# Which free PSUM bank an attention and MLP kernel takes: the one free longest in the preferred half in place of the one with the highest or lowest number

## The chip, the cores and the metric

The kernel runs on one core of a Trainium2 chip. The metric is the device time of one execution in microseconds (us), as the median of several runs.

TensorE (PE) multiplies matrices and writes the products into PSUM, an accumulator memory of eight banks; a bank holds 128 partitions of 512 fp32 numbers. VectorE (DVE) and ScalarE (ACT) read the products out of PSUM. GpSimd (POOL) helps with element-wise work, and SyncE (SP) issues the DMA transfers.

## The reference

Causal attention with a decay (8 batches, 8 heads, 576 tokens, head size 64), and then an MLP on its output, with a leaky ReLU between two matrix products:

```python
scores = scale * np.matmul(q, k.transpose(0, 1, 3, 2))
cum = np.cumsum(np.log(np.clip(f, 0.0001, 1.0)), axis=-1)
scores = np.where(causal, -1000000000.0, scores + cum[:, :, :, None] - cum[:, :, None, :])
attn = softmax(scores)                       # with 1e-09 in the sum
x = (attn @ v) as 4608 tokens of 512
h = x @ w_in                                 # 512 -> 2048
out = (max(h, 0) + alpha * min(h, 0)) @ w_out  # 2048 -> 512
```

The matrix products are made of several fp32r matmuls each (a high and a low part of either operand), so that the result has more than one pass's precision.

## The kernel before

**The stages.** Attention is cut into 32 units, each one batch and two heads. Units 0 to 9 transpose their exponentials on PE (`attention(n)`). Units 10 to 31 (`turned(n)`) transpose them on DVE (L863) and move the pieces with DMAs. A turned unit's work on PE is a first run of 18 score matmuls (`bank<-Qhl`, 64x512 and smaller), a second run of 12, and 60 matmuls that make the values (`bank<-big,vr`). DVE masks the scores (L840), ACT takes the exponentials (L820) and empties the values (L937).

**FFN1** (`ffn1(b)`, the first product of the MLP) has 9 token tiles of 512 tokens with 16 chunks each. A chunk is 12 matmuls of 128x512 at L377 (`bank<-xx,wi`), in two halves of 6, into one PSUM bank. Then the bank is read: for most tiles by ACT at L1014 and again by DVE at L1016, for the tiles of `LATE` (the first and the last two) by ACT at L1011 alone. The result `hs` goes out by a DMA. FFN1's chunks are set between the pieces of the attention units as soon as their tokens are there; after the last unit FFN1 runs alone, beside the preparation of w_out on ACT and DVE.

**FFN2** (`ffn2(u)`, the second product) has 18 units of 256 tokens. Each makes 168 matmuls of 128x256 (`bank<-wot,...` and `bank<-wi,...`) into four banks, which ACT (L1291) and DVE (L1295, L1296, L1299, L1300; in the last unit L1305 to L1308) read at the unit's end and sum.

**What sets the order.** The program is written by a planner in Python (`Plan.run`). It keeps a planned time for each engine, and in each step emits that operation which could start first by its own costs. The planned times are used only to choose; on the chip every engine runs its instructions in the emitted order and waits on semaphores. What an operation needs from a pool (a PSUM bank, a buffer) it takes when it is emitted: `Store.take(ring, now)`, where `st.free` holds pairs (planned time at which the item comes free, number). A `Ring` is one user's view of a store.

**PSUM banks.** The eight banks are one store, made of four tiles of two banks:

```python
two_banks = [psum.tile([128, 2, 512], F32, name=f"bank{i}") for i in range(4)]
banks = Store([t[:, i] for t in two_banks for i in range(2)])
rS, rT = Ring(banks, 2, 4, False), Ring(banks, 1, 3, False)
rH, rO = Ring(banks, 2, 4, True), Ring(banks, 0, 6)
rP, rV = Ring(pairs), Ring(banks, 0, 2, True)
```

Banks 0 and 1 are the first tile, 2 and 3 the second, 4 and 5 the third, 6 and 7 the fourth. The last argument is `high`: scores and transposes of the first units (`rS`, `rT`) prefer low banks, FFN1's chunks (`rH`) and the first units' values (`rV`) high ones, FFN2 (`rO`) has no preference. The framework sets the semaphore waits between operations that touch the same tile. With the first turned unit `swap_banks` takes banks 0 to 3 out of the store and gives them to the turned units as two pairs (`rP`); from there FFN1 has banks 4 to 7. `change`, after the attention, gives 0 to 3 back.

Of the kernel before, what the change touches and what calls it, by code (L numbers as in the profile page):

```python
# [48 lines left out]
class Store:  # L49
# [7 lines left out]
    def take(self, ring, now):  # L57

        near = [f for f in self.free if f[0] <= now]
        f = min(near, key=lambda f: (f[1] * (-1 if ring.high else 1))) if near and ring.high is not None else min(self.free)  # L60
        self.free.remove(f)
        return f

# [1313 lines left out]
```

## Time and profile before

| | us |
|---|---|
| median of 3 runs | 1164.29 |
| lowest and highest run | 1161.78, 1164.58 |
| the profiled execution | 1162.62 |
| its span, first to last instruction | 1160.4 |
| outside the span | 2.2 |
| PE busy | 1054.2 (91%) |
| DVE busy | 812.9 (70%) |
| ACT busy | 618.8 (53%) |
| POOL busy | 329.7 (28%) |

The mean clock that TensorE was granted is 0.997 of full speed.

How to read what follows: a chain of waits is followed back from the last instruction, at each step to what released it. "Idle before" is the time in which an engine stood still ahead of an instruction, with the instruction of another engine that ended it. A PE that is busy may still be filling or emptying its pipeline. In the names, `bank<-xx,wi` is output and inputs of an instruction, and L377 is the line of a helper through which almost all matmuls are issued, so that the operands tell the stages apart.

### The profile page before, as it was taken

How to read it: one execution, taken by the hardware profiler on the slowest of the kernel's cores; microseconds unless marked ns; L12 is line 12 of the kernel's file. 1: busy time of each engine (PE TensorE's matmuls, PEld its weight loads, DVE VectorE, ACT ScalarE, POOL GpSimd, SP SyncE). 2: the span in 40 equal slices, each digit the busy share in tenths (PEclk: the TensorE clock that was granted, in tenths of full speed). 3: DMA queues.
4: the chain of work that ended last, by engine and by line, in shares of the span. 5: the costliest groups of instructions: out<-in, count | busy, mean ns of one | idle time of the engine just before them, and what ended most of it. 6: DMA issues, size and time to landing. Idle time of an engine off the chain costs nothing.

```text
span 1160.4 us, 21964 instructions
## 1 busy us (share of the span) xinstructions
PE 1054.2 (91%) x7933; PEld 893.0 (77%) x7933; DVE 812.9 (70%) x1673; ACT 618.8 (53%) x1390; POOL 329.7 (28%) x459
## 2 busy tenths in 40 slices
PE   8889989889899989989898788889999999999998
PEld 4667767667677777777676565659899999999998
DVE  5678773657667575766665176659888898898894
ACT  5768786445454555555453154546545464545551
POOL 5577784435435353535442100000000000000000
PEclk9999999999999999999999999999999999999999
DMA  5867753666667667667666454436333434344421
GB/s 157 227 200 194 236 155 110 178 176 201 206 194 219 189 191 220 194 200 209 182 171 181 135 200 165 161 109 225 111 127 117 140 128 128 110 146 128 121 81 37
DMA packets 132879, 190.24 MB, mean 164 GB/s; under 512 B 21842, under 2 KB 78979, under 8 KB 132771
## 3 DMA queue, kind: packets, MB, share of 16 engines
q1 hardware_dynamic: 132482, 188.65, 53.4%
q8 instruction: 62, 1.02, 0.4%
q14 instruction: 47, 0.38, 0.1%
q10 hardware_dynamic: 288, 0.20, 0.1%
HBM read 103.52 MB, written 48.78 MB: 131 GB/s over the span
## 4 chain that ended last, share of the span: by engine, by line
PE 79%; DVE 10%; ACT 7%; issue 2%; DMA 1%; SPq 0%; DVEq 0%; POOL 0%; ACTq 0%; POOLq 0%
PE bank L377 76%; ACT hs L1014 2%; DVE hs L1016 2%; ACT hs L1011 2%; PE bank L586 2%; DVE big L863 1%; ACT big L582 1%; ACT big L573 1%; PE bank L437 1%; DVE big L699 1%; DMA Zt<-c 1%; DVE xx L1268 1%; DVE hs L1295 0%; PE bank L473 0%; DVE gh L1268 0%
## 5 line engine op out<-in xcount | busy, mean ns | idle before, releaser
L377 PE MATMUL bank<-xx,wi 128*128 128x512 f32 x1728 | 436.9, 401 | 77.1 <-DVE hs L1016 41.5
L377 PEld LDWEIGHTS bank<-xx,wi 128*128 128x128 f32 x1728 | 312.8, 188 | 175.2 <-DVE hs L1016 55.1
L1016 DVE SCALAR_TENSOR_TENSOR hs<-bank,sa,hs 128x512 f32<-128x512 f32 x96 | 71.5, 744 | 125.8 <-ACT hs L1014 64.8
L820 ACT ACTIVATE big<-big,st 128x512 f32<-128x512 f32 (+4 forms) x198 | 113.8, 577 | 77.6 <-DVE st L840 77.6
L541 POOL TENSOR_TENSOR Qhl<-rqk,Qhl 128x640 fp32r<-128x640 f32 (+1 forms) x56 | 87.2, 1560 | 214.8 <-ACT Qhl L540 214.8
L1014 ACT ACTIVATE hs<-bank,ab 128x512 f32<-128x512 f32 x96 | 65.9, 686 | 122.7 <-PE bank L377 107.5
L377 PE MATMUL bank<-wot,xx 128*128 128x256 f32 x1008 | 125.6, 284 | 6.1 <-DVE hs L1296 3.4
L377 PEld LDWEIGHTS bank<-wot,xx 128*128 128x128 f32 x1008 | 122.5, 192 | 7.9 <-DVE hs L1295 2.1
L377 PE MATMUL bank<-wi,xx 128*128 128x256 f32 x1008 | 124.1, 283 | 0.5 <-ACT hs L1291 0.5
L377 PEld LDWEIGHTS bank<-wi,xx 128*128 128x128 f32 x1008 | 122.3, 192 | 0.7 <-ACT hs L1291 0.7
L377 PE MATMUL bank<-Qhl 64*128 64x128 f32 (+4 forms) x840 | 97.7, 332 | 6.6 <-ACT wi L372 3.7
L377 PEld LDWEIGHTS bank<-Qhl 64*128 64x128 f32 (+1 forms) x840 | 77.0, 188 | 32.7 <-ACT xs L937 6.7
L377 PE MATMUL bank<-big,vr 128*64 128x128 f32 (+2 forms) x1880 | 97.0, 261 | 0.0
L377 PEld LDWEIGHTS bank<-big,vr 128*64 128x64 f32 x1880 | 90.1, 139 | 8.4 <-issue 4.7
L863 DVE STREAM_TRANSPOSE big<-big 128x2048 f32<-128x2048 f32 (+1 forms) x44 | 80.4, 1835 | 12.0 <-DMA big<-big 5.2
L840 DVE CUSTOM_DVE_ANT_1 big<-bank,Z 128x384 f32<-128x384 f32 (+1 forms) x88 | 39.6, 487 | 48.8 <-PE bank L377 48.8
L1265 ACT ACTIVATE xx<-gx 128x1024 fp32r<-128x1024 f32 x48 | 50.8, 1058 | 41.2 <-DVE gx L1252 27.9
L514 POOL TENSOR_TENSOR Z<-Z,tri 128x384 f32<-128x384 f32 x64 | 61.7, 968 | 29.0 <-DVE Z L498 12.1
L1011 ACT ACTIVATE hs<-bank,sg 128x512 f32<-128x512 f32 x48 | 33.0, 688 | 63.6 <-PE bank L377 59.8
L377 PE MATMUL bank<-wot,gh 128*128 128x256 f32 x504 | 63.4, 284 | 1.5 <-DVE hs L1296 0.8
L377 PEld LDWEIGHTS bank<-wot,gh 128*128 128x128 f32 x504 | 61.6, 192 | 2.4 <-DVE hs L1296 1.1
L1265 ACT ACTIVATE xx<-wx 128x256 fp32r<-128x256 f32 x68 | 33.9, 520 | 54.1 <-PE bank L377 34.2
(149 smaller groups left out, 1555.2 us busy)
## 6 DMA issues: line engine op xcount, KB each, us to landing
hd<-hs SPq DMA_DIRECT2D x144, 256.0 KB, 2.3
big<-big SPq DMA_DIRECT2D x352, 100.0 KB, 2.2
wx<-hd SPq DMA_DIRECT2D x45, 512.0 KB, 3.5
rqk<-in_qk_dram SPq DMA_DIRECT2D x28, 608.0 KB, 3.9
hr<-hd SPq DMA_DIRECT2D x27, 512.0 KB, 3.4
vr<-in_vv_dram SPq DMA_DIRECT2D x32, 320.0 KB, 3.0
big<-in_w_in_dram SPq DMA_DIRECT2D x16, 512.0 KB, 4.8
wr<-in_w_out_dram SPq DMA_DIRECT2D x16, 512.0 KB, 3.7
```

Of the source, the lines that this page charges most:

```text
L377: pe.matmul(o, lhsT, rhs, start=start, stop=stop)
L437: op("PE", 800, lambda: [pe.matmul(bw.t, wbf[:, 0:128], wbf, start=True, stop=True) for _ in range(3)], -200, [o_wbf], [bw])
L514: m1 = op("POOL", c_po(128 * 3), lambda z4=z4: po.tensor_tensor(z4()[:, 6:9], z4()[:, 0:3], tb(3), ALU.add), kc + 0.1, got + [o_mask], [bZ])
L541: o2 = op("POOL", c_po(w), lambda hi=hi, lo=lo, raw=raw: po.tensor_tensor(lo(), raw(), hi().bitcast(F32), ALU.subtract), kc, [o1], [bqk, bQ])
L586: pe.transpose(t[:, c : c + 128], src[:, 128 * j : 128 * j + 128], ident)
L820: sums.append(op("ACT", c_exp(w), lambda: ac.activation(at(), at(), AF.Exp, bias=lo()[:, col : col + 1], scale=-1.0, accum_out=su()[:, col ...
L840: ve.tensor_tensor_reduce(out=blk(e()), in0=blk(src()), in1=in1, scale=-0.125, scalar=3.0e38, op0=ALU.add, op1=ALU.min, accum_out=lo()[:, ...
L863: turns.append(op("DVE", c_tr(4 * (c1 - c0)), lambda: ve.transpose(bTt.t[:, :, c0:c1].rearrange("p k (b c) -> p k b c", c=32), bE.t[:, 4 * ...
L1011: cp = op("ACT", c_act(512), lambda bh=bh, bs=bs, fc=fc: ac.activation(bs.t, bh.t, AF.Copy, scale=sg[:, fc : fc + 1]), -1000, [last, o_sg] ...
L1014: cp = op("ACT", c_act(512), lambda bh=bh, bs=bs, fc=fc: ac.activation(bs.t, bh.t, AF.Relu, scale=ab[:, fc : fc + 1]), -1000, [last, o_sg] ...
L1016: cp = op("DVE", c_dve(512), lambda bh=bh, bs=bs, fc=fc: ve.scalar_tensor_tensor(bs.t, bh.t, sa[:, fc : fc + 1], bs.t, ALU.mult, ALU.add), ...
L1265: his.append(op("ACT", c_acs(128 * GW * (j1 - j0)), lambda j0=j0, j1=j1, src=src, o_=o_: ac.activation(o_(0, j0, j1), src(), AF.Copy), key ...
```

## The change

One line in `Store.take` is changed. It looks at the items that are free by the planned time. For a ring with a preference it took the one with the highest number (`high` true) or the lowest. Now it takes an item of the preferred half (numbers 4 to 7 for `high`, 0 to 3 otherwise) if there is one, and among these the one with the earliest planned time of coming free. Rings without a preference, and the case that nothing is free yet, are as before: the one that comes free first.

```diff
     def take(self, ring, now):
 
         near = [f for f in self.free if f[0] <= now]
-        f = min(near, key=lambda f: (f[1] * (-1 if ring.high else 1))) if near and ring.high is not None else min(self.free)
+        f = min(near, key=lambda f: ((f[1] < 4) == ring.high, f)) if near and ring.high is not None else min(self.free)
         self.free.remove(f)
         return f
```

The emitted order is the same on all engines in before and after; the bank numbers differ, and with them the waits. In the listings below bank_76 is the tile of banks 0 and 1, bank_77 that of 2 and 3, bank_78 that of 4 and 5, and bank_79 that of 6 and 7; "x11" is a count of like instructions in a row, and "[waits DVE_49]" or "[waits Activation_49]" a semaphore wait for DVE or ACT.

On PE, in a turned unit in the middle of the program, what stands between the first and the second score run (the row of `Qhl` ends each piece) is before:

```order
L377 MATMUL bank_79<-xx,wi 128x512 x12
L377 MATMUL bank_79<-xx,wi 128x512 [waits DVE_49]
L377 MATMUL bank_79<-xx,wi 128x512 x11
L377 MATMUL bank_79<-xx,wi 128x512 [waits Activation_49]
L377 MATMUL bank_79<-xx,wi 128x512 x5
L377 MATMUL bank_78<-xx,wi 128x512 x6
L377 MATMUL bank_77<-Qhl_92 128x256 [waits DVE_49]
```

and after:

```order
L377 MATMUL bank_79<-xx,wi 128x512 x6
L377 MATMUL bank_78<-xx,wi 128x512 [waits DVE_49]
L377 MATMUL bank_78<-xx,wi 128x512 x11
L377 MATMUL bank_79<-xx,wi 128x512 [waits DVE_49]
L377 MATMUL bank_79<-xx,wi 128x512 x11
L377 MATMUL bank_78<-xx,wi 128x512 [waits DVE_49]
L377 MATMUL bank_78<-xx,wi 128x512 x5
L377 MATMUL bank_77<-Qhl_92 128x256 x6
```

The 36 matmuls are the same; before, 30 of them write one tile, with a wait within it for the reader of the chunk just before, and after, the tile changes with each chunk of 12.

On PE, the end of FFN1 alone and the start of FFN2 (`wot`) is before:

```order
L377 MATMUL bank_79<-xx,wi 128x512 x11
L377 MATMUL bank_79<-xx,wi 128x512 [waits Activation_49]
L377 MATMUL bank_79<-xx,wi 128x512 x5
L377 MATMUL bank_77<-wot_6155,gh_6153 128x256 x3
L377 MATMUL bank_76<-wot_6155,gh_6153 128x256 x3
L377 MATMUL bank_78<-wot_6155,gh_6153 128x256 x3
```

and after:

```order
L377 MATMUL bank_79<-xx,wi 128x512 [waits Activation_49]
L377 MATMUL bank_79<-xx,wi 128x512 x11
L377 MATMUL bank_78<-xx,wi 128x512 [waits Activation_49]
L377 MATMUL bank_78<-xx,wi 128x512 x11
L377 MATMUL bank_77<-wot_6155,gh_6153 128x256 x6
L377 MATMUL bank_76<-wot_6155,gh_6153 128x256 x9
```

FFN1's chunks change from one tile to two in turn, and FFN2's first unit writes two tiles where it wrote three.

## Rows read from the trace of the kernel before

**Rows 1.** The page's chain, and its costliest group (busy, mean; idle before).

```profile
PE bank L377 76%; ACT hs L1014 2%; DVE hs L1016 2%; ACT hs L1011 2%; PE bank L586 2%; DVE big L863 1%; ACT big L582 1%; ACT big L573 1%; PE bank L437 1%; DVE big L699 1%; DMA Zt<-c 1%; DVE xx L1268 1%; DVE hs L1295 0%; PE bank L473 0%; DVE gh L1268 0%
...
L377 PE MATMUL bank<-xx,wi 128*128 128x512 f32 x1728 | 436.9, 401 | 77.1 <-DVE hs L1016 41.5
```

**Rows 2.** Busy time by stretch: start:end, length, engines, clock, DMA share, GB/s.

```profile
207.00:628.00 421.00, 376.74 (x2832) 296.91 (x2832) 270.81 (x606) 216.83 (x561) 182.42 (x253) 1.00 0.67 194
628.00:782.00 154.00, 124.07 (x595) 91.83 (x591) 82.57 (x140) 66.12 (x100) 8.69 (x12) 1.00 0.46 156
782.00:1160.00 378.00, 366.68 (x3025) 363.65 (x3023) 322.03 (x590) 188.29 (x329) 0.00 (x0) 1.00 0.38 123
```

**Rows 3.** What PE waits for, 207 to 628 us: total, times, longest.

```profile
PE bank L377 <- DVE hs L1016: 31.0, 24, 1.6
PE bank L377 <- ACT hs L1014: 13.2, 17, 0.8
```

**Rows 4.** The same view, 628 to 782 us.

```profile
PE bank L377 <- ACT hs L1011: 20.3, 26, 0.8
PE bank L377 <- DVE hs L1016: 9.6, 7, 1.6
```

**Rows 5.** The same view, 782 to 1160 us.

```profile
PE bank L377 <- DVE hs L1296: 4.2, 4, 1.7
PE bank L377 <- DVE hs L1295: 2.0, 4, 0.5
PE bank L377 <- DVE hs L1300: 1.1, 1, 1.1
PE bank L377 <- ACT hs L1291: 0.5, 1, 0.5
```

**Rows 6.** PE by time, 405 to 455 us: start, length [idle before].

```profile
408.50 1.77 PE L377 MATMUL bank<-Qhl 64*128 64x512 f32 x18
...
414.78 3.02 PE L377 MATMUL bank<-xx,wi 128*128 128x512 f32 x12 [1.57 <-DVE hs L1016]
418.58 3.02 PE L377 MATMUL bank<-xx,wi 128*128 128x512 f32 x12 [0.78 <-ACT hs L1014]
421.53 1.61 PE L377 MATMUL bank<-Qhl 64*128 64x256 f32 x12
...
428.95 1.77 PE L377 MATMUL bank<-Qhl 64*128 64x512 f32 x18
...
432.86 5.73 PE L377 MATMUL bank<-xx,wi 128*128 128x512 f32 x24 [0.56 <-DVE hs L1016]
```

**Rows 7.** The same view, 444 to 491 us.

```profile
445.95 1.77 PE L377 MATMUL bank<-Qhl 64*128 64x512 f32 x18
...
453.58 3.04 PE L377 MATMUL bank<-xx,wi 128*128 128x512 f32 x12 [1.56 <-DVE hs L1016]
457.39 3.06 PE L377 MATMUL bank<-xx,wi 128*128 128x512 f32 x12 [0.78 <-ACT hs L1014]
...
488.25 1.77 PE L377 MATMUL bank<-Qhl 64*128 64x512 f32 x18
```

**Rows 8.** DVE by time, 409 to 422 us.

```profile
411.64 0.71 DVE L1016 SCALAR_TENSOR_TENSOR hs<-bank,sa,hs 128x512 f32<-128x512 f32 x1
```

**Rows 9.** PE by time, 628 to 741 us.

```profile
635.21 3.02 PE L377 MATMUL bank<-xx,wi 128*128 128x512 f32 x12 [1.57 <-DVE hs L1016]
...
676.50 3.06 PE L377 MATMUL bank<-xx,wi 128*128 128x512 f32 x12 [0.78 <-ACT hs L1011]
...
722.51 11.21 PE L377 MATMUL bank<-xx,wi 128*128 128x512 f32 x48 [0.78 <-ACT hs L1011]
```

**Rows 10.** What PE waits for, 0 to 207 us.

```profile
PE bank L586 <- ACT big L582: 4.9, 6, 1.8
```

**Rows 11.** Busy time by stretch of 2 us around 176 us.

```profile
172.00:174.00 2.00, 1.33 (x7) 0.65 (x5) 1.56 (x7) 2.00 (x10) 2.00 (x5) 1.00 0.52 113
...
176.00:178.00 2.00, 2.00 (x23) 2.00 (x20) 0.00 (x0) 0.02 (x1) 0.00 (x0) 0.50 0.06 22
```

## The prediction, before the changed kernel was run

> **What bounds the kernel now.** I read the chain of work that ended last first, then the costliest groups, then the busy time by stage, then what PE waits for in each stage, and last the single rows of one period. In the chain one line of PE, L377, holds 76% of the span [rows 1]: PE is the engine that sets the end. The group of FFN1 matmuls (`bank<-xx,wi`, 128x512) stands with 77.1 us of idle time before it, 41.5 us of it ended by DVE L1016 [rows 1], and L1016 and L1011/L1014 are exactly the readers that empty FFN1's PSUM banks. By stage [rows 2]: while FFN1 runs between the pieces of the 22 `turned` units (207 to 628 us) PE is busy 376.74 of 421.00 us; while FFN1 runs alone with the preparation of w_out (628 to 782) 124.07 of 154.00; in FFN2 (782 to 1160) 366.68 of 378.00. The idle time of the first two stages is, nearly to the last tenth, the wait for those readers: 31.0 + 13.2 = 44.2 us [rows 3] and 20.3 + 9.6 = 29.9 us [rows 4]. FFN2 has 4.2 + 2.0 + 1.1 + 0.5 = 7.8 us of waits for the readers of its sums [rows 5].
>
> Why does PE wait for a reader when eight banks are there? The order shows it: a dependency is kept for a PSUM tile of two banks, not for one bank. Before, FFN1 in these stages takes bank 7, then 6, then 7: always the highest free, so nearly every matmul of FFN1 writes the tile bank_79, and each chunk waits for the reader of the chunk just before it, though that reader reads the other bank. The trace has the counter-example too. Alone, each 12 matmuls cost 3.06 us and 0.78 us of stop, or 3.02 and 1.57 where two readers follow one another [rows 9]; but at 722.51, where before's order mixes bank_78 and bank_79, 48 matmuls run in 11.21 us without a stop [rows 9].
>
> **What a stop costs.** From that row a matmul in stream costs (11.21 - 3.06) / 36 = 0.226 us, twelve cost 2.72 us, and 3.06 - 2.72 = 0.34 us of "busy" at each stop is the pipeline emptying. So a removed stop gives back its wait and about 0.34 us.
>
> **The change, part by part.** It adds and removes no instruction and the order on every engine is the same; only bank numbers differ, and with them what a matmul waits for. After, the banks of FFN1 come round as 7, 4, 6, 5: the tile changes with every chunk, and a chunk waits for the reader two chunks back.
>
> *B, FFN1 alone, 628 to 782.* There are 7 + 26 = 33 stops [rows 4]. The reader two chunks back has a whole chunk (2.72 us) in which to end, and needs 0.78 or 1.57 us [rows 9], so all stops should go: 29.9 + 33 x 0.34 = 41.1 us. I take 39, since the last values of attention and the preparation of w_out lie in the same stretch. What hid there now comes closer: DVE has 82.57 us and ACT 66.12 us of work in the 154 us [rows 2]; in 113 us that is 73% and 59%.
>
> *A, the turned units, 207 to 628.* Here the readers share DVE and ACT with attention, so I walked through one period of four units, 408.50 to 488.25 us, of 20.45 us, 17.00 us, and 42.30 us for the third and fourth together [rows 6, 7]. In the first (and the fourth alike) the three stretches of FFN1 between the two score runs have stops of 1.57 and 0.78 us [rows 6], and the second run starts 421.53 - 408.50 = 13.03 us after the first. After, these two stops go, but a new one comes: the second chunk writes bank 4 and waits for the L1016 that reads bank 5, and this L1016 stands behind a large transpose on DVE and ends at 411.64 + 0.71 = 412.35 [rows 8], 3.85 us after the unit's start. FFN1's first six matmuls end at about 1.71 + 1.36 = 3.07, so it waits about 0.87 us; then 30 matmuls follow in stream (30 x 0.226, and 0.2 to start), and the second run stands at 10.9 us: 2.1 us gained, twice in the period. From the second run to the next unit (421.53 to 428.95) PE has no stop, and I leave that as it is. In the second unit three chunks are half done at once; its stop of 0.56 us [rows 6] goes, and a wait for an L1014 that now stands behind ACT's exponentials takes its place; the ends are 0.56 us (nothing changes) and 1.57 us (a full reader's wait, the largest row of this kind), and by the walk it is nearer to the upper, 1.2: 0.35 us lost. In the third unit nothing new comes, its stops of 1.56 and 0.78 us [rows 7] go with their 0.34 each: 3.0 us gained. Sum 2.1 - 0.35 + 3.0 + 2.1 = 6.85 us in 79.75 (the fourth is taken as the first), where the rows have waits of 7.6 us: nine tenths of the waits come back. Over the stage 0.90 x 44.2 = 39.8; I take 39. Its lower end is nothing (rival 1), its upper end the waits with all 41 drains, 58.
>
> *C, FFN2, 782 to 1160.* Before, the four banks of neighbouring units share tiles (first unit 4, 0, 1, 2, second 3, 5, 7, 6); after, one unit has 0 to 3 and the next 4 to 7. The waits for L1295, L1296 and L1300, 7.3 us [rows 5], go. At the very end the last unit's third part now waits for a DVE sum on the partner bank, some 0.8 to 0.9 us in place of the 0.5 us for ACT L1291 [rows 5]. That is 6.5 to 7; I take 6.5. If DVE, busy 322.03 of 378 us [rows 2], is late with the operands instead, up to 5 of these stay.
>
> *D, the first ten units, 0 to 207.* Of FFN1's 77.1 us of idle time [rows 1] 77.1 - 44.2 - 29.9 = 3.0 lie here; I take 2. The score and transpose matmuls of these units take banks 0 to 3 by the same rule in a new order, and their waits change both ways; the nearest row is 4.9 us for ACT L582 [rows 10], so 4 either way.
>
> **Sum.** 39 + 39 + 6.5 + 2 = 86.5 us off the profiled execution's own 1162.62 us is 1076.1. The median of the runs is 1164.29, some 1.7 above, so I say 1077.
>
> **The rivals.** *1: the turned units are held by their own chain.* Values, masks, exponentials, the next score run and the moves of the transposed tiles follow one another, and when FFN1 no longer stops, PE waits for them in its place. For it: DVE 270.81 us and DMA 0.67 of the 421 us [rows 2]. Against it: between the second run and the next unit PE shows no stop now, and the unit of 17.00 us [rows 6] shows that the chain can go faster than the 20.45 before it and the 21.15 on average behind it. A falls to nothing: 1162.6 - 47.5 = 1115. *2: the preparation of w_out becomes the bound after attention.* ACT and DVE take turns in it; if their 82.57 + 66.12 = 149 us [rows 2] overlapped only half as well as needed, half of B stays: about 1095. Against it: apart, each has a quarter of the shorter stretch free. *3, slower: TensorE's clock falls.* At 172 to 174 us PE was busy 1.33 us of 2, and at 176 to 178 the granted clock was 0.50, the lower of the two levels (1.2 GHz) [rows 11]. If the new run of chunks were granted the lower level, a chunk would cost 2.72 us more; of the 144 chunks (1728 matmuls [rows 1] of 12 each) 32 eat the whole gain, and half of them make 1076 + 72 x 2.72 = 1272. Against it: the clock is 1.00 from 207 to 782 us although PE stops 74 times there [rows 2 to 4], and after the change it stops less.
>
> The Trainium skill ("TensorE: Matmul & The Clock Gate", section "A second HAM failure mode: psum-queue depth-cycling") tells of a kernel that cycles through PSUM banks each iteration, whose short idle times between matmul groups made the clock swing; by it rival 3 would come about here, since after the change FFN1 does cycle through four banks. The rows above go against it.
>
> *4: the change does nothing, since before already takes another bank for each chunk.* If what PE waits for were DVE's and ACT's own pace, not the shared tile, the stops would stay whatever the number: 1163 to 1165. Against it the 48 matmuls without a stop [rows 9]. The skill's page "Perfetto Trace Analysis" (section "Matmuls") asks for independent groups to rotate through different banks; by banks before keeps that rule already, and by its rows it does not help.
>
> **How the numbers follow.** Forecast 0.76 (1077; with A at 30 to 45, B at 30 to 41 and D at 4 either way, 1066 to 1098), rival 1 0.12, rival 2 0.07, rival 3 0.03, rival 4 0.02. The range takes in rival 2 and part of what lies between the forecast and rival 1: 1066 to 1104. A measurement of this kernel can tell about 0.3% from no change: faster than that 0.95 (forecast, 1 and 2), within it 0.02 (4), slower 0.03 (3).
>
> **What would show it.** PE's waits for L1016, L1014 and L1011 fall from 77 us in all to under 10, B's right when FFN1 alone shows 2.72 us for a chunk. A is right when the period of four units is near 73 us and the first unit of it shows one stop of 0.9 us behind L1016 of the partner bank. C is right when the waits for L1295, L1296 and L1300 are gone and one wait for DVE of under 1 us stands near the end. I am wrong if the time between the second score run and the next unit grows (rival 1), if chunks of FFN1 alone wait for w_out's ACT or DVE (rival 2), or if the granted clock of 207 to 782 us is under 1.00 (rival 3).

## The result, and the profile after

The changed kernel takes 1081.4 us (median of 4 runs, 1078.6 to 1082.9) against 1164.4 us before (4 runs): a ratio of 0.928, with an interval of 0.925 to 0.932. That is 83 us less; the forecast was 1077 us, 87 less. The profiled execution took 1082.8 us with a span of 1080.6. The mean granted clock differs a little between runs of one kernel, and the time with it: the two runs of the changed kernel at 0.991 of full speed, the profiled one among them, took 1082.8 and 1082.9 us, the two at 0.995 took 1080.0 and 1078.6.

The program falls into four stages with marks that any trace of this kernel shows: D, the first ten units and the first turned one, up to the first L905 on DVE, which stands at the end of that unit; A, the other 21 turned units (the prediction counts 22), up to the last L905; B, FFN1 alone, up to the first matmul of `wot`; C, FFN2, up to the end of the span. In us of the profiled executions, whose spans differ by 79.8 us:

| stage | before | after | gained | forecast |
|---|---|---|---|---|
| D | 207.0 | 212.9 | -5.9 | 2 (4 either way) |
| A | 420.2 | 382.6 | 37.5 | 39 |
| B | 154.9 | 117.3 | 37.6 | 39 |
| C | 378.4 | 367.8 | 10.6 | 6.5 |

The page of the changed kernel: busy time by engine, the chain by engine and by line, and the group of FFN1's matmuls (busy, mean; idle time before them and what ended most of it).

```profile
PE 1037.6 (96%) x7933; PEld 900.0 (83%) x7933; DVE 809.5 (75%) x1673; ACT 614.7 (57%) x1390; POOL 328.7 (30%) x459
...
PE 78%; DVE 10%; DMA 3%; ACT 3%; issue 3%; SPq 1%; POOL 1%; DVEq 0%; POOLq 0%; ACTq 0%
PE bank L377 75%; DVE big L863 4%; DMA big<-big 2%; PE bank L586 2%; SPq L899 1%; DVE big L840 1%; DMA Zt<-c 1%; DVE hs L1016 1%; ACT big L820 1%; PE bank L437 1%; DVE big L699 1%; ACT big L573 1%; DVE big L891 1%; ACT big L582 0%; PE bank L473 0%
...
L377 PE MATMUL bank<-xx,wi 128*128 128x512 f32 x1728 | 418.6, 396 | 15.3 <-DVE hs L1016 8.7
```

The group that had 77.1 us of idle time before it [rows 1] has 15.3, and PE's share of the span is 96%. By stretch (length; busy time of PE, PEld, DVE, ACT, POOL; clock; DMA):

```profile
213.00:596.00 383.00, 369.87 (x2830) 298.76 (x2828) 266.83 (x605) 214.06 (x561) 182.19 (x254) 1.00 0.73 213
596.00:713.00 117.00, 114.64 (x597) 94.75 (x597) 82.85 (x141) 66.22 (x101) 9.11 (x12) 1.00 0.63 210
713.00:1080.00 367.00, 363.08 (x3024) 362.68 (x3022) 321.16 (x589) 186.57 (x329) 0.00 (x0) 1.00 0.40 126
```

Against [rows 2], PE stands still for 13 us of A in place of 44, for 2 of B in place of 30 and for 4 of C in place of 11. What PE waits for, in A and then in B and C together (in total, times, longest):

```profile
PE bank L377 <- DVE hs L1016: 8.5, 10, 1.5
PE bank L377 <- ACT hs L1014: 4.7, 5, 1.2
```

```profile
PE bank L377 <- DMA big<-big: 2.1, 1, 2.1
PE bank L377 <- DVE hs L1307: 0.8, 1, 0.8
PE bank L377 <- DVE hs L1016: 0.2, 1, 0.2
```

In A, 15 waits of 13.2 us are left of 41 waits of 44.2 us [rows 3]; in B the 33 stops [rows 4] have become one of 0.2 us, and one wait for a move; in C the waits for L1295, L1296 and L1300 [rows 5] are gone, and one for L1307 has come, 0.8 us. PE by time, for the four units that answer to [rows 6, 7]:

```profile
392.18 1.77 PE L377 MATMUL bank<-Qhl 64*128 64x512 f32 x18
...
396.23 7.11 PE L377 MATMUL bank<-xx,wi 128*128 128x512 f32 x30 [0.70 <-DVE hs L1016]
403.27 1.61 PE L377 MATMUL bank<-Qhl 64*128 64x256 f32 x12
...
410.69 1.77 PE L377 MATMUL bank<-Qhl 64*128 64x512 f32 x18
...
419.18 1.66 PE L377 MATMUL bank<-xx,wi 128*128 128x512 f32 x6 [1.03 <-ACT hs L1014]
...
428.20 1.77 PE L377 MATMUL bank<-Qhl 64*128 64x512 f32 x18
429.90 10.14 PE L377 MATMUL bank<-xx,wi 128*128 128x512 f32 x42
...
447.40 1.78 PE L377 MATMUL bank<-Qhl 64*128 64x512 f32 x18
...
452.19 7.13 PE L377 MATMUL bank<-xx,wi 128*128 128x512 f32 x30 [1.45 <-DVE hs L1016]
...
466.68 1.79 PE L377 MATMUL bank<-Qhl 64*128 64x512 f32 x18
```

Between 392.18 and 410.69 one stop stands where two stood: 0.70 us, for L1016. The next unit has 1.03 us for L1014 (419.18) in place of 0.56 for L1016. The third has none: 42 matmuls run through at 429.90. The fourth has one stop again. And FFN1 alone, as in [rows 9]:

```profile
601.17 15.27 PE L377 MATMUL bank<-xx,wi 128*128 128x512 f32 x66
...
626.59 86.38 PE L377 MATMUL bank<-xx,wi 128*128 128x512 f32 x378 [0.21 <-DVE hs L1016]
712.81 5.20 PE L377 MATMUL bank<-wot,gh 128*128 128x256 f32 x42
```

378 matmuls, 31 chunks and a half, run through in 86.38 us: 2.74 us for a chunk that took 3.84 or 4.59.

### The profile page after: what moved, and what is told of

The parts are those of the page before. It is cut to its first block, busy times and chain, and to the rows that moved or that the text cites. A ratio compares the mean times of both kernels' runs of the same rounds, so it can differ in the third digit from the quotient of the medians.

```text
span 1080.6 us, 21954 instructions
## 1 busy us (share of the span) xinstructions
PE 1037.6 (96%) x7933; PEld 900.0 (83%) x7933; DVE 809.5 (75%) x1673; ACT 614.7 (57%) x1390; POOL 328.7 (30%) x459
## 4 chain that ended last, share of the span: by engine, by line
PE 78%; DVE 10%; DMA 3%; ACT 3%; issue 3%; SPq 1%; POOL 1%; DVEq 0%; POOLq 0%; ACTq 0%
PE bank L377 75%; DVE big L863 4%; DMA big<-big 2%; PE bank L586 2%; SPq L899 1%; DVE big L840 1%; DMA Zt<-c 1%; DVE hs L1016 1%; ACT big L820 1%; PE bank L437 1%; DVE big L699 1%; ACT big L573 1%; DVE big L891 1%; ACT big L582 0%; PE bank L473 0%
## 5 line engine op out<-in xcount | busy, mean ns | idle before, releaser
L377 PE MATMUL bank<-xx,wi 128*128 128x512 f32 x1728 | 418.6, 396 | 15.3 <-DVE hs L1016 8.7
L377 PEld LDWEIGHTS bank<-xx,wi 128*128 128x128 f32 x1728 | 317.1, 188 | 91.0 <-DVE hs L1016 14.6
L377 PE MATMUL bank<-wi,xx 128*128 128x256 f32 x1008 | 124.1, 283 | 0.8 <-DVE hs L1307 0.8
L377 PE MATMUL bank<-wot,xx 128*128 128x256 f32 x1008 | 123.9, 283 | 0.0
L377 PEld LDWEIGHTS bank<-wi,xx 128*128 128x128 f32 x1008 | 122.3, 192 | 1.0 <-DVE hs L1307 1.0
L377 PEld LDWEIGHTS bank<-wot,xx 128*128 128x128 f32 x1008 | 122.3, 192 | 0.0
L1016 DVE SCALAR_TENSOR_TENSOR hs<-bank,sa,hs 128x512 f32<-128x512 f32 x96 | 70.4, 738 | 55.4 <-ACT hs L1014 44.5
L377 PE MATMUL bank<-Qhl 64*128 64x128 f32 (+4 forms) x840 | 98.7, 333 | 7.1 <-DVE st L699 5.9
L377 PEld LDWEIGHTS bank<-Qhl 64*128 64x128 f32 (+1 forms) x840 | 77.8, 189 | 33.3 <-issue 10.6
L377 PE MATMUL bank<-big,vr 128*64 128x128 f32 (+2 forms) x1880 | 98.1, 263 | 2.2 <-DMA big<-big 2.1
L377 PEld LDWEIGHTS bank<-big,vr 128*64 128x64 f32 x1880 | 91.0, 140 | 10.9 <-issue 4.4
L863 DVE STREAM_TRANSPOSE big<-big 128x2048 f32<-128x2048 f32 (+1 forms) x44 | 80.4, 1835 | 20.3 <-DMA big<-big 14.6
L1014 ACT ACTIVATE hs<-bank,ab 128x512 f32<-128x512 f32 x96 | 65.4, 682 | 41.5 <-PE bank L377 29.3
L377 PE MATMUL bank<-wi,gh 128*128 128x256 f32 x504 | 62.4, 283 | 0.0
L377 PE MATMUL bank<-wot,gh 128*128 128x256 f32 x504 | 62.4, 283 | 0.0
L377 PEld LDWEIGHTS bank<-wot,gh 128*128 128x128 f32 x504 | 61.4, 192 | 0.1
L377 PEld LDWEIGHTS bank<-wi,gh 128*128 128x128 f32 x504 | 61.3, 192 | 0.0
```

The lines of the kernel that those rows point to most:

```text
L377: pe.matmul(o, lhsT, rhs, start=start, stop=stop)
L863: turns.append(op("DVE", c_tr(4 * (c1 - c0)), lambda: ve.transpose(bTt.t[:, :, c0:c1].rearrange("p k (b c) -> p k b c", c=32), bE.t[:, 4 * ...
L1014: cp = op("ACT", c_act(512), lambda bh=bh, bs=bs, fc=fc: ac.activation(bs.t, bh.t, AF.Relu, scale=ab[:, fc : fc + 1]), -1000, [last, o_sg] ...
L1016: cp = op("DVE", c_dve(512), lambda bh=bh, bs=bs, fc=fc: ve.scalar_tensor_tensor(bs.t, bh.t, sa[:, fc : fc + 1], bs.t, ALU.mult, ALU.add), ...
```

## The experiments

Kernels whose edit adds a line show later lines one higher (L378 for L377, L1017 for L1016). All were compared with runs of the kernel before on the same chip, which took 1162.6 to 1164.6 us. Stages of the profiled executions, in us:

| kernel | D | A | B | C | median | ratio to before (interval) |
|---|---|---|---|---|---|---|
| after | 212.9 | 382.6 | 117.3 | 367.8 | 1081.4 | 0.928 (0.925 to 0.932) |
| e1: old rule, banks 5 and 6 change places | 211.8 | 383.0 | 122.7 | 378.4 | 1097.4 | 0.945 (0.943 to 0.946) |
| e2: new rule, rotation through neighbours | 211.1 | 396.4 | 138.4 | 369.3 | 1117.6 | 0.962 (0.960 to 0.964) |
| e3: old rule, banks 4 to 7 as four tiles | 193.8 | 381.7 | 116.3 | 373.0 | 1067.0 | 0.919 (0.917 to 0.920) |
| e4: new rule, banks 4 to 7 as four tiles | 197.2 | 386.0 | 119.0 | 366.7 | 1070.5 | 0.921 (0.919 to 0.922) |
| e5: new rule for the high rings alone | 207.4 | 395.5 | 137.6 | 369.2 | 1113.2 | 0.956 (0.954 to 0.958) |
| e6: new rule for the low rings alone | 213.0 | 420.0 | 155.2 | 378.5 | 1170.2 | 1.005 (1.003 to 1.006) |
| e7: old rule, FFN2's units in halves | 205.9 | 420.2 | 155.4 | 369.2 | 1154.2 | 0.991 (0.989 to 0.993) |
| e8: e3 with FFN2 in halves | 194.1 | 380.6 | 118.4 | 366.7 | 1062.3 | 0.913 (0.911 to 0.914) |
| e9: e8 with the new rule for the high rings | 195.6 | 384.5 | 117.4 | 366.7 | 1065.7 | 0.916 (0.913 to 0.919) |
| e10: e4 with FFN1's stores on POOL | 202.3 | 364.8 | 115.7 | 366.8 | 1051.3 | 0.904 (0.901 to 0.907) |
| e11: e8 with FFN1's stores on POOL | 196.6 | 372.4 | 115.1 | 366.7 | 1056.7 | 0.909 (0.907 to 0.911) |
| e12: before with FFN1's stores on POOL | 214.0 | 418.4 | 154.8 | 378.5 | 1168.2 | 1.005 (1.003 to 1.006) |

### The tile, or the rest of the bank?

Two theories fit the result: that the tile of two banks made PE wait, or that a bank had rested too little when it was taken again. e1 and e2 tell them apart with the plan held: only the places of the numbers change.

e1, in the kernel before:

```diff
     banks = Store([t[:, i] for t in two_banks for i in range(2)])
+    banks.items = [banks.items[i] for i in (0, 1, 2, 3, 4, 6, 5, 7)]
```

> The rule and the plan of before, but banks 5 and 6 change places, so that the two banks that FFN1 takes in turn (numbers 7 and 6) lie in two tiles. Theory 1 (a wait is kept per tile of two banks, and the new rule gains because neighbouring chunks change the tile): nearly all of what the new rule gained in 207 to 782 us comes back with the old rule, some 37 + 37 us; the stops of 0.78 us in FFN1 alone are gone; FFN2 keeps its waits of some 7 us; 1085 to 1100 us. Theory 2 (the gain comes from the rule's aim, a bank that has rested longest; four banks in turn in place of two): as before, 1160 to 1167 us, stops of 0.78 and 1.57 us as before.

Measured 1097.4 us, as the tile theory has it. The old rule still takes mostly two numbers in turn, but they lie in two tiles now, and A is 383.0 us, as with the new rule. FFN1 alone on PE:

```profile
634.98 42.45 PE L378 MATMUL bank<-xx,wi 128*128 128x512 f32 x186 [0.78 <-ACT hs L1012]
...
680.66 37.01 PE L378 MATMUL bank<-xx,wi 128*128 128x512 f32 x162 [0.78 <-ACT hs L1012]
```

186 and 162 matmuls run through. The few stops of 0.78 us that are left in B stand where, in the built program, the old rule takes a third bank, which is now a partner of the first. C stays as before, 378.4 us.

e2, in the changed kernel:

```diff
     banks = Store([t[:, i] for t in two_banks for i in range(2)])
+    banks.items = [banks.items[i] for i in (0, 1, 2, 3, 6, 4, 5, 7)]
```

> The new rule and its plan, but banks 4 to 7 change places so that its rotation of four banks runs through the tiles as fourth, fourth, third, third: the rest of each bank is the same, only the partner in the tile is another. Theory 1 (per tile): every second chunk of FFN1 stops for the reader of the chunk just before it; about half of the 75 us gained in 207 to 782 us goes: 1110 to 1130 us, and in FFN1 alone two chunks of every four show a stop of 0.78 us. Theory 2 (longest rest): the time of the new rule, 1077 to 1084 us.

Measured 1117.6 us, in the range of the tile theory. Every bank rests as long as in the changed kernel, and yet FFN1 alone stops after each 24 matmuls, which are two chunks:

```profile
666.89 5.73 PE L378 MATMUL bank<-xx,wi 128*128 128x512 f32 x24 [0.83 <-ACT hs L1012]
673.40 5.78 PE L378 MATMUL bank<-xx,wi 128*128 128x512 f32 x24 [0.78 <-ACT hs L1012]
679.95 5.74 PE L378 MATMUL bank<-xx,wi 128*128 128x512 f32 x24 [0.78 <-ACT hs L1012]
```

e3 and e4 take the shared tile away where FFN1 works, with the old and the new rule:

```diff
-    two_banks = [psum.tile([128, 2, 512], F32, name=f"bank{i}") for i in range(4)]
-    banks = Store([t[:, i] for t in two_banks for i in range(2)])
+    two_banks = [psum.tile([128, 2, 512], F32, name=f"bank{i}") for i in range(2)]
+    one_bank = [psum.tile([128, 512], F32, name=f"bank{i}") for i in range(4, 8)]
+    banks = Store([t[:, i] for t in two_banks for i in range(2)] + [t[:, :] for t in one_bank])
```

> The rule and the plan of before, but banks 4 to 7 are four tiles of one bank each. Theory 1 (per tile): FFN1 waits only for the reader of its own bank, two chunks back, the stops of FFN1 alone go, 1080 to 1098 us. Theory 2 (longest rest): 1160 to 1167 us.

Measured 1067.0 us: the old rule without the shared tile is faster than the new rule with it, and faster than expected, since D gains 13 us too (193.8 for 207.0). So what cost the kernel before its time in A and B was the shared tile and not the old rule by itself. In A PE still waits, now for an earlier reader of its own bank:

```profile
PE bank L378 <- DVE hs L1017: 13.0, 13, 2.4
```

> The new rule with banks 4 to 7 as four tiles of one bank each. Theory 1 (per tile): the 13.2 us that PE still waits for L1016 and L1014 in the turned units (banks 4 and 5, or 6 and 7, share a tile there) and the 0.8 us for L1307 at the end go; if nothing else is late 1081 - 13 - 0.8 - 15 drains of 0.34 = 1062 us, and with the moves of the transposed tiles late in some of the units (L863 waits for them already) 1066 to 1076 us. Rival (the turned units are at the pace of their own chain and moves): 1078 to 1083 us, with PE waiting for DMA or DVE L863 in its place.

Measured 1070.5 us. The waits for L1016 and L1014 and the one for L1307 are gone as expected; but A takes 386.0 us, no less than the 382.6 of the changed kernel, which is the rival's case for that stage. The time came out in the first theory's range all the same, because D is 197.2 where 212.9 was counted. PE's wait in A is another now, for DVE's masks of the second score run:

```profile
PE bank L378 <- DVE st L841: 19.3, 23, 1.4
```

### What holds the turned units at 381 to 386 us

after, e1, e3, e4, e8 and e9 all have A between 380.6 and 386.0 us, with different waits of PE. What they share is that DVE's transposes (L863, here L864) wait for the moves of the piece before: 12 to 19 us of A in after, e1, e3 and e8, and over 50 in e4 and e9. Before and in e4 (total, times, longest):

```profile
DVE big L863 <- DMA big<-big: 4.8, 4, 1.8
```

```profile
DVE big L864 <- DMA big<-big: 50.8, 17, 4.2
```

DVE by time shows one such wait:

```profile
379.80 2.31 DVE L864 STREAM_TRANSPOSE big<-big 128x2048 f32<-128x2048 f32 x1 [2.78 <-DMA big<-big]
...
395.37 0.21 DVE L906 STREAM_TRANSPOSE st<-st 128x32 f32<-128x32 f32 x1
398.81 2.31 DVE L864 STREAM_TRANSPOSE big<-big 128x2048 f32<-128x2048 f32 x1 [3.22 <-DMA big<-big]
```

After the end of a unit (L906) DVE stands still for 3.22 us until the moves of the piece before (`big<-big`) have landed, and only then starts the next transpose; the masks stand behind it. Those moves are issued by SP, one after the other:

```profile
385.94 5.39 SPq L900 DMA_DIRECT2D big<-big  x7
391.42 0.53 SPq L1019 DMA_DIRECT2D hd<-hs  x1
392.00 2.42 SPq L900 DMA_DIRECT2D big<-big  x4
394.51 0.53 SPq L1019 DMA_DIRECT2D hd<-hs  x1
395.08 1.78 SPq L900 DMA_DIRECT2D big<-big  x3
```

Seven issues fill 5.39 us, four 2.42, and between them stand FFN1's stores (`hd<-hs`) of 0.53 us each. A store is issued in order and can first have to wait for its reader, and what stands behind it waits too; in A of e4 SP's waits of this kind are:

```profile
SPq L1019 <- DVE hs L1017: 15.4, 14, 1.9
```

e10 takes those stores from SP, at the same places of the plan:

```diff
-            hd_ops[b, fc] = op("SP", 400, lambda bs=bs, fc=fc: sy.dma_start(
+            hd_ops[b, fc] = op("SP", 400, lambda bs=bs, fc=fc: (sy if b in LATE[1:] else po).dma_start(
```

> The new rule with one-bank tiles (e4_single_after), but FFN1's stores of the tiles that run beside attention are issued by POOL in place of SP, at the same places of the plan. In e4 PE no longer waited for a reader of a shared tile in the turned units, yet these took 386 us, with 19 us of waits for L841 behind transposes that wait for the moves SP issues. Theory A (the turned units are now at the pace of SP's queue: 85% issuing): the waits for L841 fall by half or more and the turned units come to 365 to 378 us, the time to 1050 to 1063 us. Theory B (the chain of masks, exponentials and transposes itself, or the transfers, set that pace): 383 to 388 us for the turned units, 1068 to 1073 us. If POOL is held up by the stores' waits: slower than 1075 us.

Measured 1051.3 us: A falls to 364.8 us, and PE is busy for all of it (length; PE, PEld, DVE, ACT, POOL; clock; DMA):

```profile
202.00:567.00 365.00, 364.99 (x2832) 300.73 (x2831) 267.88 (x605) 211.62 (x560) 229.13 (x339) 1.00 0.77 225
```

DVE's wait for the moves is down to a quarter:

```profile
DVE big L864 <- DMA big<-big: 13.6, 12, 2.0
```

So in e4 it was the stores in SP's queue, not the chain of masks and exponentials. The edit changes one thing more: by its page the stores' data go over another DMA queue than before (q0, 29.37 MB, where q1 carried them), so that the order of issue and the order of transfers were not told apart by a run of their own. Against the transfers speaks that a move took longer from issue to landing in e10, 3.1 us in place of 2.2 (medians of the pages). That the queue also holds up after, e1 and e3 is argued from DVE's waits; only e4 and e8 (below) were tried without the stores. e12 is the control, the same edit in the kernel before:

> A control: the kernel before with only that move of the stores to POOL. If the shared tile sets the pace of the turned units there, and SP's queue does so only once the tile's waits are gone: no gain, 1160 to 1168 us, the waits for L1016 and L1014 within 3 us of the 31.0 and 13.2 of before. If SP's queue held the turned units in the kernel before too: 1140 to 1152 us.

Measured 1168.2 us, at the upper end of the first case, with next to nothing gained in A (418.4 for 420.2) and the waits of [rows 3]:

```profile
PE bank L377 <- DVE hs L1016: 31.5, 24, 2.5
PE bank L377 <- ACT hs L1014: 13.2, 17, 0.8
```

While the shared tile sets A's pace, taking the stores from the queue gains nothing. (What e12 loses lies in D, 214.0 for 207.0; e10's D is 5 us longer than e4's as well. POOL has other work there that the stores may hold up; this was not taken apart.)

### Which half of the change did what

e5, in the changed kernel, leaves the old rule to the low rings:

```diff
-        f = min(near, key=lambda f: ((f[1] < 4) == ring.high, f)) if near and ring.high is not None else min(self.free)
+        f = min(near, key=lambda f: ((f[1] < 4, f) if ring.high else f[1:])) if near and ring.high is not None else min(self.free)
```

> The new rule for the rings that prefer the high half (FFN1, values of the first units), the old rule (lowest number) for scores and transposes of the first ten units. If the 5.9 us that the first stage (0 to 207 us before, 0 to 213 after) lost come from the low rings: that stage is back at about 207 us and the time is 1074 to 1077 us. If they come from the high rings or from falls of the granted clock alone: the stage stays at 211 to 213 us and the time at 1079 to 1083 us. The other stages as with the new rule (382.6, 117.3 and 367.8 us).

Measured 1113.2 us, a miss of over 30 us, and the most telling one. D is back at 207.4 us, as the first case has it (more on this below). But A and B are 13 and 20 us longer than in the changed kernel, though FFN1 follows the same rule in both. FFN1 alone on PE looks like e2:

```profile
661.54 5.73 PE L377 MATMUL bank<-xx,wi 128*128 128x512 f32 x24 [0.83 <-ACT hs L1011]
668.05 5.78 PE L377 MATMUL bank<-xx,wi 128*128 128x512 f32 x24 [0.78 <-ACT hs L1011]
674.60 5.78 PE L377 MATMUL bank<-xx,wi 128*128 128x512 f32 x24 [0.78 <-ACT hs L1011]
```

The built program says why: FFN1's banks come round as 4, 5, 6, 7 there, so that two neighbours share a tile, and as 7, 4, 6, 5 in the changed kernel. Whichever order the banks come free in when the rotation starts is kept for nearly all of FFN1, since each chunk takes the bank that was given back first. The low rings, whose rule alone differs between the two kernels and which reach into the upper half when theirs is full, set that order. So 33 of the 75 us that the changed kernel gains in A and B hang on the order into which its rotation happened to fall.

e6, in the kernel before, gives the new rule to the low rings alone:

```diff
-        f = min(near, key=lambda f: (f[1] * (-1 if ring.high else 1))) if near and ring.high is not None else min(self.free)
+        f = min(near, key=lambda f: ((-f[1],) if ring.high else (f[1] >= 4, f))) if near and ring.high is not None else min(self.free)
```

> The other half of the change: the new rule for scores and transposes of the first units alone, the old rule for FFN1. The turned units, FFN1 alone and FFN2 as before (420, 155 and 378 us). If the low rings lose the 5.9 us: 1168 to 1171 us; if not: 1161 to 1166 us.

Measured 1170.2 us, 5.6 more than before, and D 213.0 us, as the first case has it. But D hides two things in one number, since it ends with the first turned unit. PE begins that unit's first score run at 188.0 us before, 197.1 after, 194.0 in e6 and 190.2 in e5. So the ten first units alone, with the same matmuls to within two of 1350, lost 9.1 us in the changed kernel, 6.0 with the low rings' half (e6) and 2.2 with the high rings' half (e5); the first turned unit gave back 3.2 in the changed kernel and 1.8 in e5. The ten units in before, after, e6 and e5 (length; PE, PEld, DVE, ACT, POOL; clock; DMA):

```profile
0.00:188.00 188.00, 169.45 (x1350) 127.00 (x1350) 126.11 (x313) 137.54 (x373) 128.21 (x184) 0.98 0.63 189
0.00:197.10 197.10, 174.08 (x1350) 130.71 (x1350) 127.62 (x313) 137.88 (x373) 127.97 (x186) 0.96 0.59 180
0.00:194.00 194.00, 170.88 (x1348) 128.99 (x1348) 128.47 (x313) 137.46 (x373) 127.59 (x186) 0.96 0.61 183
0.00:190.20 190.20, 171.11 (x1349) 128.84 (x1350) 126.47 (x313) 137.71 (x373) 128.40 (x186) 0.96 0.62 186
```

PE's idle time (length less busy time) is 18.6 us before, 23.0 after, 23.1 in e6 and 19.1 in e5: the new rule for the low rings costs 4.5 us of waits, and that for the high rings 0.5. The greatest part is for DVE L699, the mask of the first units' scores, before:

```profile
PE bank L377 <- DVE st L699: 3.8, 4, 2.0
```

and in e6 (the first line stands in the changed kernel too, word for word):

```profile
PE bank L377 <- DVE st L699: 8.2, 6, 2.4
...
PE bank L651 <- DVE st L699: 1.6, 1, 1.6
```

The rest of the loss is busy time for the same matmuls, 4.6 us more after, 1.4 in e6 and 1.7 in e5, with a granted clock of 0.96 in place of 0.98. This part differs between runs of one kernel, too: see the pairs of runs at 0.991 and 0.995 above, and e1, which has the old rule, a clock of 0.95 by the same view up to its first turned unit, and a D of 211.8 us. Waits and clock can go together, since the clock fell behind a stretch in which PE waited before as well (busy 1.33 us of 2, and 2 us later a granted clock of 0.50 [rows 11]).

e7 gives FFN2's units the lower and the upper four banks in turn, and nothing else:

```diff
-        f = min(near, key=lambda f: (f[1] * (-1 if ring.high else 1))) if near and ring.high is not None else min(self.free)
+        f = min(near, key=lambda f: (f[1] * (-1 if ring.high else 1))) if near and ring.high is not None else min(self.free, key=lambda f: (ring.most == 6 and (f[1] < 4) == (ring.next // 4 % 2), f))
```

> The old rule for all rings with a preference; FFN2 alone is changed: its units take the lower and the upper four banks in turn. The 7.3 us of waits for L1295, L1296 and L1300 go with some 3 us of drains (13 stops): FFN2 takes 367 to 369 us in place of 378.4, all else as before, 1152 to 1155 us. If FFN2's gain in the changed kernel came from its earlier start and another place of its loads instead: 1161 to 1165 us.

Measured 1154.2 us, as expected: C is 369.2 us, and the stops between units are gone. Three waits are left in C, two of 0.5 us and at the end one for a sum, on a shared tile as in the changed kernel:

```profile
PE bank L377 <- DVE hs L1308: 0.8, 1, 0.8
```

### Putting the best of each stage together

e8 is e3 with e7's line; e9 is e8 with e5's line for the high rings; e11 is e8 with e10's stores.

> The old rule, banks 4 to 7 as four tiles of one bank, and FFN2's units in the lower and the upper four banks in turn: the best of each stage so far put together. 193.5 us for the first units, 382 for the turned ones, 116.5 for FFN1 alone, 367 for FFN2 and 2.2 outside: 1061 us (1058 to 1064). If FFN2's part does not add to the other: 1066 to 1068 us.

Measured 1062.3 us, and 194.1, 380.6, 118.4 and 366.7 us by stage: the gains add up.

> One-bank tiles for 4 to 7, FFN2 in halves as in e8, and the new rule for the high rings with the old one for the low rings. If with one-bank tiles a longer rest of FFN1's banks is worth something: up to 10 us under e8, 1050 to 1059 us. If the tile was all, as e3 against e4 suggests: the time of e8 within some 5 us, 1058 to 1067 us, the turned units at 382 to 386 us.

Measured 1065.7 us: the second case. With one-bank tiles and SP's queue in the way, a longer rest gains nothing.

> e8 (old rule, one-bank tiles, FFN2 in halves) with FFN1's stores beside attention issued by POOL, as in e10: the best of each stage. If the gains add up: 194 + 365 + 117 + 366.7 + 2.2 = 1045 us (1041 to 1049). If POOL, which prepares tables and quotients for the first units, is held up by the stores there (e10's first stage took 202 us against e4's 197): 1049 to 1055 us.

Measured 1056.7 us, outside both ranges: the gains do not add up, and the cause named for that case, POOL in the first units, has little part in it (D 196.6 us, against 194.1 in e8). A is 372.4 us, not 365. DVE's wait for the moves is nearly gone (2.7 us, against 17.7 in e8), but with the old rule, which mostly takes two banks in turn, PE waits for an earlier reader of the same bank, also with one-bank tiles:

```profile
PE bank L378 <- DVE hs L1017: 5.2, 6, 1.4
```

e10, which has the new rule, has no such wait. So a longer rest does pay in the end, some 8 us of A, once both the tile and SP's queue are out of the way. By the median the fastest kernel run is e10, at 1051.3 us, though its four runs (1048.2 to 1056.2) overlap with those of e11 (1052.6 to 1058.8). e10 with the old rule for the low rings was not tried; D was 6 to 7 us shorter in e9 and e11, which have that rule.

## Why the prediction was right, point by point

The forecast of 1077 us came within 5 us of the measured 1081.4, by the mechanism that it names in A, B and C. Part of the closeness is luck: C gained 4.1 us more than forecast, which made up for half of what D fell short.

- **The mechanism** (a wait per tile of two banks, and neighbouring chunks that change the tile) is shown from both sides: e1 gains without the rule, e2 and e5 lose with it, e3 needs no rule. (That nearly every matmul of FFN1 wrote one tile before is put too strongly: in the built program it is four fifths.)
- **A**: 39 forecast, 37.5 measured. The walk through the period holds in the stretch that it describes best: in the changed kernel's four units from 264.5 to 337.4 us (second, third, fourth and first of the pattern, from one L905 to the next) the lengths are 17.28, 18.88, 18.36 and 18.40 us, where the walk gives 17.35, 18.85, 18.35 and 18.35. In the period shown above they are 18.51, 17.51, 19.20 and 19.28: there L863 starts late behind the moves, and so the stop for L1016 is 1.45 us (452.19) and not 0.87. For the second unit the walk is right by two slips that cancel: it put the wait for L1014 at 1.2 us in place of a stop of 0.56, which would lose 0.64 us and not the 0.35 that it states. The wait measured 0.84 us at 272.24 us, and that unit lost 0.28 us.
- **B**: 39 forecast, 37.6 measured. All 33 stops went but 0.2 us, and a wait of 2.1 us for a move came in the last units. The price of a stop, its wait and 0.34 us of busy time, is right: 2.74 us a chunk.
- **C**: 6.5 forecast, 10.6 measured. The waits went as forecast, and the new one at the end is 0.84 us, as forecast. The step that was mis-sized is the busy time that a stop adds: it was counted for A and B at 0.34 us a stop and left out for C. Ten stops [rows 5] went and one came: 9 x 0.34 = 3.1 us as an estimate (PE's busy time in C fell by 3.6, from 366.68 to 363.08), and 7.0 us of waits in place of the 6.5 taken, make 10.1 of the 10.6. (The 13 stops in what was expected of e7 are a miscount.)
- **D**: a gain of 2 forecast, a loss of 5.9 measured, outside the 4 either way. This is the term that failed, and it failed in its second half. FFN1's waits went about as forecast: the first turned unit gained 3.2 us. "Their waits change both ways" was bounded by one row, the 4.9 us for L582, which hardly changed (5.2 after); the waits for L699 doubled instead, and the granted clock fell a little, so that the ten first units lost 9.1 us. About half of that, 4.5 us, is waits, which e6 shows to come from the low rings' rule. The other half is busy time at a lower clock, and e1 shows the clock to fall without that rule too.
- **"Under 10 us" of FFN1's waits** were promised; 15.3 us are left. That contradicted the walk itself, which had 0.9 us in two units of four and 1.2 in a third, some 15 us over 21 units.
- **Rival 1** (the turned units' own chain) stood for all of A lost, with 0.12. e4 and e10 show that such a limit is real, but it lies at 381 to 386 us, about where the change came to rest, and in e4 it is SP's queue with FFN1's stores in it and not the chain of masks and exponentials. The change was within a few us of meeting it: without the waits for its tiles, in e4, A was no shorter.
- **Rivals 2 and 3**: B runs through with the preparation of w_out beside it, and the clock is 1.00 in each of the three stretches from 213 us on. The Trainium skill ("TensorE: Matmul & The Clock Gate", section "A second HAM failure mode: psum-queue depth-cycling") tells of a kernel that cycles through PSUM banks, whose frequent short idle times made the clock swing; here it did not, neither with four banks in turn nor, with 74 stops between the chunks, before [rows 2 to 4].
- **What the prediction did not see**: that the good order 7, 4, 6, 5 was read from the built program and does not follow from the rule. It was right for this program; e5 shows that the same rule for FFN1 with another start gives 1113 us.

## What to carry to other kernels

When PE waits for a reader, look at which tile that reader reads and not only at which bank: a tile of two banks makes neighbours of accumulations that have nothing to do with each other, and one tile to a bank (e3) gained more here than the new rule did. A rule that takes what came free first keeps whatever order it starts with, so where tiles are shared the order must be laid down, not found. And price a stop of PE with the busy time that it adds, here 0.34 us on top of the wait, in every stage.

## What the runs showed that was not expected

- SP's issue of a move takes about 0.6 to 0.8 us here (4 in 2.42 us, 7 in 5.39). In A of e4 there are some 25 issues to a unit (16 moves, 4 stores, 5 or 6 loads and small ones), and they fill 326 of the 386 us. Taking four stores per unit away from SP was worth 21 us of A (e4 to e10), though each move then took longer to land.
- The banks of the first ten units mattered too: one-bank tiles for 4 to 7 shortened D by 13 us (e3), a stage in which FFN1's own waits were only 3.0 us.
